# Eight PSUM banks handed out one or two at a time, and mask set-up moved to the front, in a planned attention + MLP kernel

## The chip, the cores and the metric

The kernel runs on one core of a Trainium2 chip. A time is the device time of one execution in microseconds. A "span" is the time from the first to the last instruction in a profile; it is about 1.8 us shorter than the time of the same execution.

## The reference

The reference is attention over 4 batches, 8 heads, 768 rows and 64 columns per head, with a local window of 96 keys and 8 global keys, followed by an MLP whose activation is h - tanh(h).

```
scores = q @ k^T / sqrt(64) - slope[head] * distance        # distance is |row - key|, 96 for far global keys
keep   = key < 8  or  0 <= row - key < 96
a      = softmax(where(keep, scores, -1e9))
x      = (a @ v) laid out as [4*768 rows, 8*64 columns]     # 3072 x 512
h      = x @ w_in                                           # 512 x 2048
out    = (h - tanh(h)) @ w_out                              # 2048 x 512, float32
```

## The kernel before

The work is cut into 24 units u, each one batch and 128 rows. A unit goes through these steps:

- T: k and q are transposed, on TensorE (PE) for the first 8 units and by a DMA transpose for the rest.
- B, S: the bias and the scores, one matmul group each. E: exp. From unit 3 on there is no B, and M multiplies by a mask that was made once (mk, mke).
- AV: probabilities times v. R: division by the sum.
- X: x is transposed, on PE for the first 9 units; from unit 9 on a DMA transpose on the SP queue does it (`a_DX`).
- m1, th, g, m2: the MLP.

A function `plan()` holds assumed durations of every operation and lists them in order of a simulated time. Each engine then executes its operations strictly in that order. So a change of buffers or of priorities moves instructions all over the kernel.

```
    ps_big = ctx.enter_context(tc.tile_pool(name="ps_big", bufs=2, space=bass.MemoryType.PSUM))   # 2 x two banks
    ps_one = ctx.enter_context(tc.tile_pool(name="ps_one", bufs=4, space=bass.MemoryType.PSUM))   # 4 x one bank
    ...
    def a_mk(m, a):
        mkp[m, a] = ps_one.tile([P, 512], FP32, name="one")
        bias(mkp[m, a], m, a, True)
    ...
    def a_DX(u):
        nc.sync.dma_start_transpose(out=x_dst(u), in_=xs[u].rearrange("q h d -> q (h d)"))
    ...
    SLACK_DT, SLACK_DX = 5.0, 2.0          # what the plan adds to a DMA transpose of k,q and of x
    LOADS = "tttiiiitiitoooiotoiooot"      # t: k, q, v of one unit; i: a piece of w_in; o: of w_out
    ...
        if u == 0:
            op(("ident",), POOL, 0.3, unit, after=[("issue", prev)])
            op(("nums",), POOL, 0.7, numbers, after=[("issue", ("ident",))])
    ...
    for h in range(H):
        eng = DVE if h < 2 else ACT
        op(("sl", h), eng, 0.14 if h < 2 else 0.22, lambda h=h, eng=eng: slope(h, eng), after=[("ident",)], pri=-3)
    ...
            op(("mk", m, a), PE, 0.22, lambda m=m, a=a: a_mk(m, a), after=biased_by + [("dT", 1), ("AV", 1)],
               take=["one"], pri=1)
    ...
        op(("R", u), DVE, 0.8, lambda u=u: a_R(u), after=[("AV", u)], take=["x"], give=["big"])
        b, at, n_b = block_of(u)
        xdep = ("Xe", u - 1) if at else None          # none for the first unit of a block
        ...
            op(("Xe", u), SP, 0.2, lambda u=u: a_DX(u), after=[("R", u), xdep],
               take=xtake, give=["x"], dma=T_DX, slack=SLACK_DX)
    ...
            op(("m1", g, f), PE, ..., after=[("Xe", us[-1]), ("in", (f + m - 1) // FJ)], take=["one"], pri=2, ...)
```

The softmax here doesn't subtract the row's maximum and nothing guards it: scores larger than these inputs give would overflow.

## Time and profile before

| | before |
|---|---|
| median of the runs, us | 217.36 (217.12 to 217.69) |
| span of the profiled run, us | 215.3 |
| PE busy | 208.8 us, 97% |
| VectorE, ScalarE busy | 61%, 59% |
| start of the first matmul, end of the last | 1.3 us, 212.0 us |

The first fence is from the page of the kernel before: the span, the busy times, the busy tenths of PE and of the DMA engines in 40 equal slices, and the share of each engine in the chain of work that ended last.

```profile
span 215.3 us, 5039 instructions
PE 208.8 (97%) x2031; PEld 127.3 (59%) x2031; DVE 132.3 (61%) x279; ACT 127.3 (59%) x214; POOL 72.0 (33%) x92
PE   6997999999999999999999999999999999999993
DMA  6999999999999999999999999226242011101112
PE 90%; DMA 4%; POOL 4%; issue 0%; DVE 0%; POOLq 0%
```

PE is full in nearly every slice after the fourth. What is lost is lost early, and the DMA engines are full until about 130 us. The next fence is the start of the chain of the kernel before. Its columns are the start in us, the length in us, and what it was.

```profile
9.38 8.14 DMA kq<-in_k_dram
17.52 0.04 issue
17.57 0.63 PE one L254 x8
```

The chain comes to the load of unit 3's k, which lands at 17.52 us, and after it there is almost only PE. The waits view of the kernel before gives PE's wait for this load. Its columns are the engine and line, what it waited for, us in all, times, and the longest. The second line, of POOL: the loads of k wait for a free buffer until a DMA transpose has read the old one.

```profile
PE one L254 <- DMA kq<-in_k_dram: 1.1, 1, 1.1
POOL kq L218 <- DMA qk<-kq: 36.8, 7, 7.9
```

**A measure used below: lost time.** For every matmul that computes something (warm-up matmuls left out) take its columns at 2.4 GHz, and at least 29.2 ns, close to the 29 to 30 ns at which the 65-column matmuls follow one another in this trace (median and mean within a group). The sum is 202.5 us, the same in all kernels here. Lost time at t is t less the needed work done by then, counting every matmul whose weight load has started except the last one. I read it from the starts of the weight loads, one for each matmul, because no record of these is missing (2031 here). It is good to about 0.2 us, the length of one 512-column matmul. A PE wait shows as a jump in lost time. A difference of lost time between two kernels is a lead of one over the other. In the kernel before it is 9.34 us at 24 us and 9.13 us at 208 us: from 24 us on PE loses nothing.

### The profile page before, as it was taken

The page shows a single profiled execution, that of the slowest core. Times are in us where ns is not written, and L with a number is a line of the kernel's source. Part 1 is how long each engine was busy: PE and PEld are TensorE (multiplying, and loading weights), DVE is VectorE, ACT ScalarE, POOL GpSimd, SP SyncE. Part 2 cuts the span into 40 slices and gives each one's busy share as a digit, 9 for nine tenths or more (in the row PEclk, how much of TensorE's full clock was granted, in tenths as well). Part 3 has the DMA queues.
Part 4 walks back from the last instruction along what each step waited for, and adds up shares of the span by engine and source line. Part 5 has one row for each costly group of instructions (what it writes and reads, how often), then busy time and mean ns, then how long its engine had stood idle before and what let it go on. Part 6 is the DMA issues. An engine that isn't in the chain of part 4 may idle for free.

```text
span 215.3 us, 5039 instructions
## 1 busy us (share of the span) xinstructions
PE 208.8 (97%) x2031; PEld 127.3 (59%) x2031; DVE 132.3 (61%) x279; ACT 127.3 (59%) x214; POOL 72.0 (33%) x92
## 2 busy tenths in 40 slices
PE   6997999999999999999999999999999999999993
PEld 1755996877745655455655655555555555555453
DVE  5555986759544889448878755766756644444311
ACT  5677998556543786536775655777477454434310
POOL 8976768698445354041354130000000000000000
PEclk9999999999999999999999999999999999999999
DMA  6999999999999999999999999226242011101112
GB/s 161 197 197 176 196 183 201 159 187 140 161 163 190 160 156 183 149 206 156 127 100 129 140 116 195 59 73 51 85 110 74 16 61 49 44 8 49 49 53 99
DMA packets 103960, 26.95 MB, mean 125 GB/s; under 512 B 92416, under 2 KB 100992, under 8 KB 103936
## 3 DMA queue, kind: packets, MB, share of 16 engines
q0 software_dynamic: 74048, 13.11, 80.0%
q1 hardware_dynamic: 26032, 6.95, 22.1%
q10 hardware_dynamic: 3856, 6.56, 9.3%
q8 instruction: 16, 0.26, 0.5%
q14 instruction: 8, 0.07, 0.1%
HBM read 27.26 MB, written 6.29 MB: 156 GB/s over the span
## 4 chain that ended last, share of the span: by engine, by line
PE 90%; DMA 4%; POOL 4%; issue 0%; DVE 0%; POOLq 0%
PE one L372 39%; PE one L404 39%; PE big L287 5%; DMA kq<-in_k_dram 4%; PE big L311 3%; PE big L315 2%; POOL w_in_bf L225 1%; POOL vb L212 1%; PE one L250 1%; PE one L338 1%; POOL kq L216 1%; PE one L254 1%; PE one L141 0%; POOL over L106 0%; POOL dist L106 0%
## 5 line engine op out<-in xcount | busy, mean ns | idle before, releaser
L372 PE MATMUL one<-xT,w_in_bf 128*128 128x128 bf16 (+1 forms) x768 | 96.7, 273 | 0.0
L404 PE MATMUL one<-w_out_bf,g 128*128 128x512 bf16 (+2 forms) x416 | 95.0, 363 | 0.0
L389 DVE TENSOR_TENSOR g<-one,th 128x384 bf16<-128x384 f32 (+1 forms) x120 | 67.7, 580 | 34.8 <-ACT th L383 32.6
L383 ACT ACTIVATE th<-one 128x384 f32<-128x384 f32 (+1 forms) x120 | 60.4, 516 | 43.3 <-PE one L372 39.5
L372 PEld LDWEIGHTS <-w_in_bf 128*128 128x128 bf16 x768 | 58.4, 98 | 29.3
L404 PEld LDWEIGHTS <-g 128*128 128x128 bf16 x416 | 37.9, 98 | 33.9
L218 POOL DMA_DIRECT2D kq<-in_k_dram x20 | 17.8, 891 | 40.7 <-DMA qk<-kq 36.8
L295 ACT ACTIVATE pd<-big 128x1024 bf16<-128x1024 f32 x24 | 24.6, 1024 | 7.9 <-PE big L287 7.9
L212 POOL DMA_DIRECT2D vb<-in_v_dram x24 | 21.6, 899 | 4.0 <-DMA qk<-kq 1.4
L298 DVE TENSOR_TENSOR pd<-pd,mk 128x1024 bf16<-128x1024 bf16 x21 | 14.5, 690 | 12.8 <-ACT pd L295 12.8
L295 ACT ACTIVATE po<-big 128x1024 bf16<-128x1024 f32 x20 | 20.5, 1027 | 0.5 <-PE big L287 0.5
L414 ACT COPY ot<-one 128x512 f32<-128x512 f32 x18 | 10.5, 585 | 15.7 <-PE one L404 15.7
L218 POOL DMA_DIRECT2D kq<-in_q_dram x20 | 17.7, 887 | 4.6 <-DMA vb<-in_v_dram 3.8
L324 DVE TENSOR_TENSOR x<-big,rden 128x512 bf16<-128x512 f32 x24 | 16.6, 691 | 0.8
L287 PEld LDWEIGHTS <-qk 64*128 64x128 bf16 x352 | 10.0, 94 | 8.6 <-issue 7.4
L287 PE MATMUL big<-qk 64*128 64x128 bf16 x352 | 14.4, 218 | 0.0
L311 PE MATMUL big<-vb,pd 128*128 128x65 bf16 x192 | 14.0, 193 | 0.2 <-ACT po L295 0.2
L298 DVE TENSOR_TENSOR po<-po,mk 128x1024 bf16<-128x1024 bf16 x18 | 12.4, 689 | 2.9 <-ACT po L295 2.9
L311 PEld LDWEIGHTS <-pd 128*128 128x128 bf16 x192 | 12.6, 97 | 2.0
L315 PE MATMUL big<-vb,po 128*128 128x65 bf16 x160 | 12.4, 193 | 0.0
L315 PEld LDWEIGHTS <-po 128*128 128x128 bf16 x160 | 10.4, 97 | 1.7 <-issue 0.2
L414 DVE COPY ot<-one 128x512 f32<-128x512 f32 (+2 forms) x8 | 4.5, 558 | 8.5 <-PE one L404 8.5
(45 smaller groups left out, 86.2 us busy)
## 6 DMA issues: line engine op xcount, KB each, us to landing
out_dram<-ot ACTq DMA_DIRECT2D x23, 256.0 KB, 2.9
vb<-in_v_dram POOLq DMA_DIRECT2D x24, 128.0 KB, 7.9
kq<-in_k_dram POOLq DMA_DIRECT2D x22, 128.0 KB, 8.1
kq<-in_q_dram POOLq DMA_DIRECT2D x22, 128.0 KB, 7.9
w_in_bf<-in_moe_w_in_dram POOLq DMA_DIRECT2D x8, 256.0 KB, 7.7
w_out_bf<-in_moe_w_out_dram POOLq DMA_DIRECT2D x8, 256.0 KB, 8.6
kf<-in_k_dram SPq DMA_DIRECT2D x2, 256.0 KB, 4.9
qf<-in_q_dram ACTq DMA_DIRECT2D x2, 256.0 KB, 3.8
```

Source lines behind the costliest of these rows:

```text
L212: i = nc.gpsimd.dma_start(out=vb[u % NV][:, :, 0:Dh], in_=by_head)
L218: i = nc.gpsimd.dma_start(out=dst.rearrange("p (h d) -> p h d", d=Dh), in_=by_head)
L287: nc.tensor.matmul(s[:, slot(2 * p + hh), :], qk[u - o][r, 1, p, :], qk[u][r, 0, p, :], start=u >= BIASED, stop=True, skip_group_check=u < ...
L295: nc.scalar.activation(pr[u, o], s, AF.Exp, bias=0.0, scale=scale)
L298: nc.vector.tensor_tensor(out=pr[u, o], in0=pr[u, o], in1=mk[:, :, mask_of(u, o), :], op=ALU.mult)
L311: nc.tensor.matmul(dst, pr[u, 0][:, slot(h), :], vb[u % NV][:, h, :], start=True, stop=last,)
L315: nc.tensor.matmul(dst, pr[u, 1][:, slot(h), :], vb[(u - 1) % NV][:, h, :], start=False, stop=True,)
L324: nc.vector.tensor_tensor(out=xs[u].rearrange("q (a h) d -> q a h d", a=2), in0=t[:, :, :, 0:Dh], in1=rden.to_broadcast([P, 2, H // 2, Dh] ...
L372: nc.tensor.matmul(t[:, (f - f0) * n : (f - f0 + 1) * n], w_in_bf[j][:, c, fo : fo + P], xT[b][:, c, o : o + n], start=(c == 0), stop=(c = ...
L383: nc.scalar.activation(h_view(ths[g, f0], g), h_view(hs[g, f0], g), AF.Tanh, bias=0.0, scale=1.0)
L389: nc.vector.tensor_tensor(out=gs[b][:, f0 : f0 + m, o : o + n], in0=h_view(hs.pop((g, f0)), g), in1=h_view(ths.pop((g, f0)), g), op=ALU.su ...
L404: nc.tensor.matmul(os_[u, part][:, 0 : hi - lo], gs[b][:, f, t * P : (t + 1) * P], w_out_bf[f // FJ][:, f % FJ, lo:hi], start=(f == 0), st ...
```

## The change

The intent: let any free bank, or any two adjacent ones, serve any use, so that the order of work is not held by the split into 2 two-bank and 4 one-bank buffers; make the positions and the identity before the first load of v, the slopes all on VectorE, and two of the three masks at once; and so start the dense stretch of PE earlier. A few assumed durations in `plan()` change too. The diff, cut to its core:

```diff
-    ps_big = ctx.enter_context(tc.tile_pool(name="ps_big", bufs=2, space=bass.MemoryType.PSUM))
-    ps_one = ctx.enter_context(tc.tile_pool(name="ps_one", bufs=4, space=bass.MemoryType.PSUM))
+    ps_pool = ctx.enter_context(tc.tile_pool(name="ps_pool", bufs=1, space=bass.MemoryType.PSUM))
+    NB = 8
+    ps = ps_pool.tile([P, NB, 512], FP32, name="ps")
+    banks = {}
+    def one(key):
+        return ps[:, banks[key], :]
+    def two(key):
+        return ps[:, banks[key] : banks[key] + 2, :]
 ... every user takes one(key) or two(key); take/give of "one" and "big" become hold/free of a key
-    LOADS = "tttiiiitiitoooiotoiooot"
+    LOADS = "tttiiiitiitoooiootiooot"
+    op(("ident",), POOL, 0.3, unit)
+    op(("nums",), POOL, 0.7, numbers, after=[("issue", ("ident",))])
+    prev = ("nums",)
-        if u == 0:
-            op(("ident",), POOL, 0.3, unit, after=[("issue", prev)])
-            op(("nums",), POOL, 0.7, numbers, after=[("issue", ("ident",))])
-            prev = ("nums",)
-        eng = DVE if h < 2 else ACT
-        op(("sl", h), eng, 0.14 if h < 2 else 0.22, lambda h=h, eng=eng: slope(h, eng), after=[("ident",)], pri=-3)
+        op(("sl", h), DVE, 0.12, lambda h=h: slope(h), after=[("ident",)], pri=-3)
-            op(("mk", m, a), PE, 0.22, ..., after=biased_by + [("dT", 1), ("AV", 1)], take=["one"], pri=1)
+            op(("mk", m, a), PE, 0.22, ..., after=biased_by + [("dT", 1), None if m else ("AV", 4)],
+               hold=[(("mk", m, a), 1)], pri=1)
 ... in plan(): the two pools are replaced by the times at which each bank is free
+        def find(hold):
+            got, at, b = {}, 0.0, list(bank)
+            for label, n in hold:
+                if n == 1:
+                    w, i = min((max(b[i], at), -i) for i in range(NB))
+                    i = -i
+                else:
+                    w, i = min((max(b[i], b[i + 1], at), i) for i in range(NB - 1))
+                ...
```

Not in the diff, because it follows from the plan: PE's order, and the times at which everything is issued, differ in the whole kernel.

More of the change, by code (lines that the diff above doesn't have):

```diff
@@ L88, with one_bf @@
     zero = cpool.tile([P, 512], BF16, name="zero")
+    NB = 8
[3 more added lines that the diff above has]
+        return ps[:, banks[key], :]
+    def one_bf(key):
+        return one(key).bitcast(BF16)
+    def two(key):
+        return ps[:, banks[key] : banks[key] + 2, :]
     w_in_bf = [cpool.tile([P, CD, FJ * P], BF16, name=f"w_in_bf{j}") for j in range(WJ)]
@@ L129, in distance_1, with slope @@
         nc.vector.memset(dT[:, 2, 0:G], float(L))
-    def slope(h, eng):
-        f = -(2.0 ** (-8.0 * (h + 1) / H)) / scale
-        if eng is ACT:
-            nc.scalar.activation(slopes[:, slot(h), :], ident, AF.Copy, bias=0.0, scale=f)
-        else:
-            nc.vector.tensor_scalar(
-                out=slopes[:, slot(h), :], in0=ident, scalar1=f, scalar2=None, op0=ALU.mult
-            )
+    def slope(h):
+        nc.vector.tensor_scalar(
+            out=slopes[:, slot(h), :], in0=ident, scalar1=-(2.0 ** (-8.0 * (h + 1) / H)) / scale,
+            scalar2=None, op0=ALU.mult,
+        )
     def bias(dst, m, a, stop):
@@ L148, in a_mk @@
     def a_mk(m, a):
-        mkp[m, a] = ps_one.tile([P, 512], FP32, name="one")
+        mkp[m, a] = one(("mk", m, a))
         bias(mkp[m, a], m, a, True)
@@ L166, in copy_on, with op @@
         return {ACT: nc.scalar.copy, DVE: nc.vector.tensor_copy, POOL: nc.gpsimd.tensor_copy}[eng]
-    def op(key, eng, us, fn, after=(), take=(), give=(), pri=0, dma=0.0, alt=None, at=None, slack=0.0):
+    def op(key, eng, us, fn, after=(), take=(), give=(), hold=(), free=(), pri=0, dma=0.0, alt=None, at=None, slack=0.0):
         ops[key] = dict(
             key=key, at=at, slack=slack, eng=eng, us=us, fn=fn, alt=alt, after=[a for a in after if a is not None],
-            take=list(take), give=list(give), pri=pri, dma=dma,
+            take=list(take), give=list(give), hold=list(hold), free=list(free), pri=pri, dma=dma,
         )
@@ L240, in a_T @@
         if u < APART or j == 1:
-            tr[u, j] = ps_one.tile([P, 2, NP, P], BF16, name="one")
+            tr[u, j] = one_bf(("T1" if j else "T", u)).rearrange("p (j n f) -> p j n f", j=2, f=P)
         else:
@@ L274, in a_B @@
     def a_B(u, o):
-        sc[u, o] = ps_big.tile([P, 2, 512], FP32, name="big")
+        sc[u, o] = two(("S", u, o))
         for a in range(2):
@@ L281, in a_S @@
             if u >= BIASED:
-                sc[u, o] = ps_big.tile([P, 2, 512], FP32, name="big")
+                sc[u, o] = two(("S", u, o))
             s = sc[u, o].rearrange("q a (h f) -> q (a h) f", f=P)
@@ L305, in a_AV @@
     def a_AV(u):
-        av[u] = ps_big.tile([P, 2, 512], FP32, name="big")
+        av[u] = two(("AV", u))
         t = av[u][:, :, 0 : (H // 2) * (Dh + 1)].rearrange("q a (h d) -> q a h d", d=Dh + 1)
@@ L335, in a_X @@
         x = xs[u].rearrange("q h d -> q (h d)")
-        tr[u, "x"] = ps_one.tile([P, CD, P], BF16, name="one")
+        tr[u, "x"] = one_bf(("X", u))[:, 0 : CD * P].rearrange("p (c f) -> p c f", f=P)
         for c in range(CD):
@@ L353 @@
     gs, hs, ths, os_, ots = {}, {}, {}, {}, {}
-    warm_bank = []
     def shape1(g):
@@ L361, in warm @@
     def warm():
-        if not warm_bank:
-            warm_bank.append(ps_one.tile([P, 512], FP32, name="one"))
-        nc.tensor.matmul(warm_bank[0], zero[:, 0:P], zero, start=True, stop=True)
+        nc.tensor.matmul(ps[:, NB - 1, :], zero[:, 0:P], zero, start=True, stop=True)
     def m1(g, f0):
         b, o, n, m = shape1(g)
-        t = hs[g, f0] = ps_one.tile([P, 512], FP32, name="one")
+        t = hs[g, f0] = one(("m1", g, f0))
         for f in range(f0, f0 + m):
@@ L400, in m2 @@
         if qq == 0:
-            os_[u, part] = ps_one.tile([P, DM], FP32, name="one")
+            os_[u, part] = one(("m2", u, part))
         b, t, _ = block_of(u)
@@ L422 @@
     AHEAD = 5.5
+    INF = 1.0e9
+    NUDGE = {}
     SLACK_DT, SLACK_DX = 5.0, 2.0
@@ L431, with load @@
             n_of[c] += 1
-    prev = None
-    def load(key, us, fn, dma, after=(), take=()):
+    op(("ident",), POOL, 0.3, unit)
+    op(("nums",), POOL, 0.7, numbers, after=[("issue", ("ident",))])
+    prev = ("nums",)
+    def load(key, us, fn, dma, after=(), take=(), slack=0.1):
         nonlocal prev
-        op(key, POOL, us, fn, after=[prev and ("issue", prev)] + list(after), take=take, dma=dma)
+        op(key, POOL, us, fn, after=[prev and ("issue", prev)] + list(after), take=take, dma=dma, slack=slack)
         prev = key
@@ L455 @@
             load(key, 0.7 if rows else 0.88, lambda u=u, nm=nm: load_bf(u, nm), T_ROWS if rows else T_LD,
-                 after=after, take=["kq"] if nm == "kf" else [])
-        if u == 0:
-            op(("ident",), POOL, 0.3, unit, after=[("issue", prev)])
-            op(("nums",), POOL, 0.7, numbers, after=[("issue", ("ident",))])
-            prev = ("nums",)
-    op(("dT", 0), DVE, 1.0, distance_0, after=[("nums",)], pri=-2)
+                 after=after, take=["kq"] if nm == "kf" else [], slack=1.0 if u == PLAIN + 1 else 0.15)
+    op(("dT", 0), DVE, 1.2, distance_0, after=[("nums",)], pri=-2)
     op(("dT", 1), DVE, 0.6, distance_1, after=[("nums",), ("issue", ("dT", 0))], pri=-1)
     for h in range(H):
-        eng = DVE if h < 2 else ACT
-        op(("sl", h), eng, 0.14 if h < 2 else 0.22, lambda h=h, eng=eng: slope(h, eng), after=[("ident",)], pri=-3)
+        op(("sl", h), DVE, 0.12, lambda h=h: slope(h), after=[("ident",)], pri=-3)
     biased_by = [("dT", 0)] + [("sl", h) for h in range(H)]
@@ L482 @@
         for a in range(2):
-            op(("mk", m, a), PE, 0.22, lambda m=m, a=a: a_mk(m, a), after=biased_by + [("dT", 1), ("AV", 1)],
-               take=["one"], pri=1)
+            op(("mk", m, a), PE, 0.22, lambda m=m, a=a: a_mk(m, a), after=biased_by + [("dT", 1), None if m else ("AV", 4)],
+               hold=[(("mk", m, a), 1)], pri=1)
             op(("mke", m, a), ACT, 0.52, lambda m=m, a=a: a_mke(m, a), after=[("mk", m, a)],
-               give=["one"], pri=1)
+               free=[("mk", m, a)], pri=1)
     for u in range(NU):
@@ L498 @@
             t_us = 0.47 if PLAIN <= u < ROWS else 0.24
-            two = u < APART
+            apart = u < APART
             for j, r in ((1, rk), (0, rq)):
                 prior = [("issue", ("T1", u))] if j == 0 else []
-                op(("T1" if j else "T", u), PE, t_us, lambda u=u, j=j: a_T(u, j), after=[r] + late + prior,
-                   take=["one"] if two or j else [], give=[] if j else ["kq"])
+                name = ("T1" if j else "T", u)
+                op(name, PE, t_us, lambda u=u, j=j: a_T(u, j), after=[r] + late + prior,
+                   hold=[(name, 1)] if apart or j else [], give=[] if j else ["kq"])
                 flex(("Te", u, j), [(ACT, 0.5), (DVE, 0.6 if u < ROWS else 0.34)],
                      lambda eng, u=u, j=j: a_Te(u, j, eng),
-                     after=[("T1" if j and two else "T", u)] + ([] if two or j else [("Te", u, 1)]),
-                     give=["one"] if two or not j else [])
+                     after=[("T1" if j and apart else "T", u)] + ([] if apart or j else [("Te", u, 1)]),
+                     free=[name] if apart else [] if j else [("T1", u)])
         else:
@@ L517 @@
                                     ("issue", ("B", u, 0) if o else ("S", u - 1, 0)) if u or o else None],
-                   take=["big"])
+                   hold=[(("S", u, o), 2)])
                 op(("S", u, o), PE, 0.43, lambda u=u, o=o: a_S(u, (o,)),
@@ L522 @@
             op(("S", u, 0), PE, 0.65 if i else 0.43, lambda u=u, os=os: a_S(u, os),
-               after=te + [kdep], take=["big"] * len(os))
+               after=te + [kdep], hold=[(("S", u, o), 2) for o in os])
         for o in os:
             op(("E", u, o), ACT, 0.93, lambda u=u, o=o: a_E(u, o), after=[("S", u, o if u < BIASED else 0)],
-               take=["p%d" % o], give=["big"])
+               take=["p%d" % o], free=[("S", u, o)])
             if u >= BIASED:
@@ L535 @@
            after=[(pm, u, 0), (pm, u, 1) if i else None, rv, ("V", u - 1) if i >= 2 else None],
-           take=["big"], give=["p0", "p1"] if i else ["p0"])
-        op(("R", u), DVE, 0.8, lambda u=u: a_R(u), after=[("AV", u)], take=["x"], give=["big"])
+           hold=[(("AV", u), 2)], give=["p0", "p1"] if i else ["p0"])
+        op(("R", u), DVE, 0.8, lambda u=u: a_R(u), after=[("AV", u)], take=["x"], free=[("AV", u)])
         b, at, n_b = block_of(u)
@@ L541 @@
         if u < PE_X:
-            op(("X", u), PE, 0.23, lambda u=u: a_X(u), after=[("R", u)], take=["one"], give=["x"])
+            op(("X", u), PE, 0.23, lambda u=u: a_X(u), after=[("R", u)], hold=[(("X", u), 1)], give=["x"])
             flex(("Xe", u), [(DVE, 0.34), (ACT, 0.5)], lambda eng, u=u: a_Xe(u, eng),
-                 after=[("X", u), xdep], take=xtake, give=["one"])
+                 after=[("X", u), xdep], take=xtake, free=[("X", u)])
         else:
@@ L553 @@
             op(("m1", g, f), PE, CD * m * (n / 2400.0 + 0.0025), lambda g=g, f=f: m1(g, f),
-               after=[("Xe", us[-1]), ("in", (f + m - 1) // FJ)], take=["one"], pri=2,
+               after=[("Xe", us[-1]), ("in", (f + m - 1) // FJ)], hold=[(("m1", g, f), 1)], pri=2,
                give=["xT"] if f + m == CF and end_b else [])
@@ L558 @@
             op(("g", g, f), DVE, 0.06 + 1.05 * w, lambda g=g, f=f: m1_g(g, f), after=[("th", g, f)],
-               take=["g"] if f == 0 and b else [], give=["one", "th"], pri=2)
+               take=["g"] if f == 0 and b else [], give=["th"], free=[("m1", g, f)], pri=2)
     for u in range(NU):
@@ L568 @@
                after=[("out", (4 * qq + 3) // FJ), ("g", g, (4 * qq + 3) // m * m)],
-               take=(["one", "mo"] if u < EARLY2 else ["one"]) if qq == 0 else [],
+               take=["mo"] if u < EARLY2 and qq == 0 else [], hold=[(("m2", u, part), 1)] if qq == 0 else [],
                give=["g"] if n == n_u - 1 and u >= N0 and u % HT == (N0 + HT - 1) % HT else [], pri=2)
@@ L574 @@
                  after=[("m2", u, 4 * part + 3)], take=["ot"] if part == 0 else [],
-                 give=["one", "mo"] if u < EARLY2 else ["one"], pri=1)
+                 give=["mo"] if u < EARLY2 else [], free=[("m2", u, part)], pri=1)
             op(("st", u, part), SP if u == NU - 1 else ACT, 0.1 if u == NU - 1 else 0.4, lambda u=u, part=part: store(u, part), after=[("ev", u, part)],
@@ L580, in plan @@
     def plan():
-        bufs = {"big": 2, "one": 4, "mo": 3, "kq": KQ, "p0": 3, "p1": 3,
+        bufs = {"mo": 3, "kq": KQ, "p0": 3, "p1": 3,
                 "x": 3, "xT": 3, "g": 3, "th": 3, "ot": 4}
         avail = {n: [0.0] * c for n, c in bufs.items()}
-        free = {PE: WARM[0], ACT: 2.8, DVE: 1.5, POOL: 0.85, SP: 0.7}
-        avail["one"][0] = WARM[1]
+        free = {PE: WARM[0], ACT: 3.4, DVE: 1.5, POOL: 1.2, SP: 0.7}
+        bank = [0.0] * NB
+        bank[NB - 1] = WARM[1]
+        def find(hold):
[6 more added lines that the diff above has]
+                    w, i = min((max(b[i], b[i + 1], at), i) for i in range(NB - 1))
+                if w == INF:
+                    return None, None
+                at, got[label] = w, i
+                b[i : i + n] = [INF] * n
+            return at, got
         ring = {SP: [0.0, []], POOL: [5.7, []]}
         share = {SP: 0.35, POOL: 0.65}
-        done, start = {}, {}
+        done, start, width = {}, {}, {}
         f1 = f2 = 0.0
@@ L627, in plan @@
                     continue
+                if o["hold"]:
+                    w = find(o["hold"])[0]
+                    if w is None:
+                        continue
+                    t = max(t, w)
                 for p in set(o["take"]):
@@ L635, in plan @@
                     continue
-                c = (round(t, 3), o["pri"], n)
+                c = (round(t + NUDGE.get(key, 0.0), 3), o["pri"], n)
                 if best is None or c < best[0]:
@@ L661, in plan @@
                 done[key] = end + LAT[o["eng"]]
+            if o["hold"]:
+                for b in range(NB):
+                    if bank[b] < t:
+                        bank[b] = t
+                got = find(o["hold"])[1]
+                banks.update(got)
+                for label, n in o["hold"]:
+                    bank[got[label] : got[label] + n] = [INF] * n
+                    width[label] = n
+            for label in o["free"]:
+                bank[banks[label] : banks[label] + width[label]] = [done[key]] * width[label]
             for p in o["take"]:
```

## The prediction

> **What bounds the kernel now.** TensorE: the page gives PE 208.8 of 215.3 us (97%) at full granted clock, VectorE 61%, ScalarE 59%. I summed every matmul's streamed columns at 2.4 GHz, warm-up matmuls left out: 201.7 us of needed work. The Trainium skill ("TensorE: Matmul & The Clock Gate", Back-to-back issue gap) gives N/2.4 + 2.5 ns per matmul; the trace agrees (four 512-column matmuls start every 0.86 us). From 20 us to the end the start-to-start gaps sum to about nothing: PE is dense. All that is lost is lost before: PE starts at 1.3 us, and up to 20 us only 10.7 us of needed work runs; the rest is 11 warm-up matmuls and waits.
>
> The waits view names the largest: 1.1 us of PE for the kq load of unit 3. In the chain of waits this load is the long piece, 9.38 to 17.52 us, and PE alone follows it. The POOL queue's loads land one after another, 0.9 to 1.3 us apart, from 7.3 to 40 us, with DMA at 9 tenths in the slices. So the end is "landing of a load + all PE work that stands behind it". For unit 3's k: 17.52 + (201.75 - 8.54) = 210.7 us, the highest of all loads; the last matmul ended at 212.0 (1.3 us[...] on top), the span at 215.3.
>
> **What the change does.** No work is added or removed: same 2031 matmuls, loads, evictions (six slopes move from ScalarE, where they took 1.3 us, to VectorE, about 0.15 us each). It moves work:
> - Positions and identity come before the first v load: bias ready at most 0.2 us earlier (4.6 to 4.4), since all slopes now precede the distances on VectorE.
> - Four mask matmuls and their exps come at 5 us instead of 14 to 20. ScalarE keeps 13 to 17 us for the exps of unit 2, so its second exp (16.7 us) comes about 1.6 us earlier, and AV of unit 2 with it. The first exp is delayed about 0.3 us (7.6 to 8.0).
> - With eight banks on demand three score tiles and an AV tile can stand at once.
> - PE's order as built: before unit 3's k transpose 11.1 us of needed work instead of 8.5 (masks, AV 2, X 2, two more MLP chunks). Its bound falls to 208.2.
>
> The same sum for every load, new order, old landings: the second w_out load (26.75 us, with 19.2 us of work before it, formerly 24.1) gives 209.3, the highest; the k loads of units 3 and 4, w_in 7 and later kq loads crowd at 208.2 to 208.9. So 210.7 falls to 209.3: 1.4 us. The loads cap it: a larger gain up front only waits for them. The tail (3.3 us from last matmul to end) is unchanged.
>
> **Prediction.** 216.0 us, range 214.9 to 217.2. Faster by over 2%: 0.02; within 2%: 0.96; slower by over 2%: 0.02.
>
> **What would show it.** Needed PE work before 20 us up from 10.7 to 12 us or more; no 1.1 us wait for kq of unit 3, but 0.5 to 1 us for w_out at 25 to 27 us; landings within 0.5 us of before; last matmul at about 210.5; same busy times.
>
> **What would make it wrong.** One PSUM tile making waits between unrelated banks (I saw none in the built order); early masks on ScalarE delaying the first scores more; a new hole after 30 us where PE, now ahead, waits for exps or loads; that w_out load landing later.

## More of the kernel before

From unit 6 on, three units form one block, and the first matmul of the block's m1 needs all three transposes of x.

`xdep` makes the plan put the transpose of x of a unit behind the planned landing of the one before it in the same block. The first unit of a block has no such condition. Units 9 to 11 are one block, and unit 12 begins the next. In the order that comes out, the transpose of unit 12 stands before that of unit 11 on the SP queue.

## The result, and the profile after

| | before | after |
|---|---|---|
| median, us | 217.36 | 217.22 (216.87 to 217.53) |
| ratio, 95% interval | | 0.9992 (0.9972 to 1.0012) |
| needed work done by 20 us, us | 10.66 | 11.89 |
| lost time at 24 us | 9.34 | 8.27 |
| lost time at 88 us | 9.45 | 8.17 |
| lost time at 104 us | 9.21 | 9.75 |
| end of the last matmul, us | 212.02 | 212.41 |

A ratio is the mean time of one kernel's fast runs over the mean of the other's in the same rounds, so it isn't quite the ratio of the medians quoted beside it. All outputs are right.

The time is the same. The table tells where it went: the kernel after leads by 1.1 us at 24 us and 1.3 us at 88 us, and has lost all of it, and 0.5 us more, by 104 us. The same lines of the page of the kernel after:

```profile
span 215.7 us, 5020 instructions
PE 208.0 (96%) x2005; PEld 127.5 (59%) x2031; DVE 132.3 (61%) x286; ACT 126.0 (58%) x207; POOL 71.9 (33%) x92
PE   7999999999999999988999999999999999999993
DMA  5999999999999999999999624323042021101112
PE 96%; issue 2%; DVE 1%; DVEq 0%
```

PE's fourth slice is now full. But there are two 8s, slices 18 and 19, about 92 to 102 us. A caution: this profile lacks 26 of PE's 2031 matmul records, and each missing one looks like a gap of about 0.2 us, so small gaps and the busy sum are not to be trusted here; the weight loads are all there. The chain of the kernel after, near those slices (start, length, what):

```profile
95.48 0.86 PE ps L409 x4
96.34 1.32 issue
97.67 3.41 PE ps L377 x20
```

And the first line of PE's waits in the kernel after:

```profile
PE ps L377 <- issue: 1.3, 1, 1.3
```

There is one wait of 1.3 us, before the first m1 matmul (L377) of the block of units 9 to 11, and the wait of 1.1 us for unit 3's k is gone. The profile calls the new wait "issue": it names no releaser. What the matmul waits for in the program are the three transposes of x of its block. So look at the last of them to be issued, unit 11's, on the SP queue. The view is of the tile xT on SP; the first line gives the time of the issue (ns, then start in us), the second the time from issue to landing. In the kernel before:

```profile
L350 SPq DMA_TRANSPOSE xT<-x x1: 1257/1257/1257, 88.8 to 88.8; - x1
DMA to landing us min/median/max: 5.3/5.3/5.3
```

And in the kernel after:

```profile
L358 SPq DMA_TRANSPOSE xT<-x x1: 1257/1257/1257, 88.7 to 88.7; - x1
DMA to landing us min/median/max: 8.9/8.9/8.9
```

In both kernels it is issued at 88.7 to 88.8 us. Before, it landed at 94.02 us, and PE came to it only at 95.92 us, as its timeline shows:

```profile
95.92 2.12 PE L372 MATMUL one<-xT,w_in_bf 128*128 128x384 bf16 x12
```

After, it landed at 97.58 us, and PE had come at 96.34 us and started at 97.67 us. So PE did not reach this matmul earlier than before: in the new order 1.3 us more needed work stands ahead of it. What makes the wait is that the landing moved by 3.6 us, more than the 1.9 us that it had to spare. So two things are to be explained: why a transpose whose data were ready at 86.14 us (the end of R of unit 11) was issued at 88.7, and why it then took 8.9 us.

For the first, the SP queue has unit 12's transpose ahead of it. VectorE's timeline in the kernel after has the ends of R of units 11 and 12 (start plus length):

```profile
85.45 0.69 DVE L332 TENSOR_TENSOR x<-ps,rden 128x512 bf16<-128x512 f32 x1
86.75 0.69 DVE L332 TENSOR_TENSOR x<-ps,rden 128x512 bf16<-128x512 f32 x1
```

So unit 12's transpose was issued at 87.47 us, and one transpose holds the queue for 1.2 us, as the first line of the view of xT shows. For the second, POOL issues the loads of unit 19 at about that time in the kernel after, and much later in the kernel before. The timeline of POOL, with start, length, line, and the idle time before it and its releaser, in the kernel before:

```profile
85.14 0.89 POOL L212 DMA_DIRECT2D vb<-in_v_dram  x1
92.56 0.88 POOL L218 DMA_DIRECT2D kq<-in_k_dram  x1 [6.53 <-DMA qk<-kq]
```

And in the kernel after, where the last three are the loads of unit 19 (the first line of each fence is unit 18's v):

```profile
84.69 0.90 POOL L220 DMA_DIRECT2D vb<-in_v_dram  x1
87.33 0.88 POOL L226 DMA_DIRECT2D kq<-in_k_dram  x1 [1.74 <-DMA qk<-kq]
88.19 0.89 POOL L226 DMA_DIRECT2D kq<-in_q_dram  x1
89.68 0.88 POOL L220 DMA_DIRECT2D vb<-in_v_dram  x1 [0.60 <-issue]
```

The loads come 5.2 us earlier, because unit 14's DMA transpose of k and q, which frees their buffer, was issued at 76.6 us instead of 83.1. The Trainium skill ("DMA: Bandwidth & Descriptors", Issuing engines are not separate DMA queues) says that transfers started from different engines run on the same 16 DMA engines and interleave; if so, these loads would slow the transpose. That has to be tested. The windows view of 88 to 98 us shows the cost in PE's busy time (columns: window, us, then busy time and count of PE, PEld, DVE, ACT, POOL, then granted clock, DMA share, GB/s), first in the kernel before:

```profile
88.00:98.00 10.00, 10.00 (x91) 5.23 (x89) 4.16 (x9) 5.21 (x8) 2.63 (x3) 1.00 1.77 176
```

And in the kernel after, where PE is busy 1.4 us less:

```profile
88.00:98.00 10.00, 8.63 (x81) 4.41 (x81) 5.45 (x12) 3.99 (x5) 1.96 (x3) 1.00 2.11 174
```

### The profile page after: what moved, and what is told of

Its sections match the earlier page's. It is cut to its first block, busy times and chain, and to the rows that moved or that the text cites. A ratio compares the mean times of both kernels' runs of the same rounds, so it can differ in the third digit from the quotient of the medians.

```text
span 215.7 us, 5020 instructions
## 1 busy us (share of the span) xinstructions
PE 208.0 (96%) x2005; PEld 127.5 (59%) x2031; DVE 132.3 (61%) x286; ACT 126.0 (58%) x207; POOL 71.9 (33%) x92
## 4 chain that ended last, share of the span: by engine, by line
PE 96%; issue 2%; DVE 1%; DVEq 0%
PE ps L377 39%; PE ps L409 38%; PE ps L295 6%; PE ps L319 3%; PE ps L323 2%; PE ps L149 2%; PE ps L369 2%; PE ps L258 2%; PE ps L346 1%; PE ps L262 1%; DVE x L332 0%; DVE ot L419 0%; DVE zero L736 0%; DVE rden L331 0%; DVE ident L735 0%
## 5 line engine op out<-in xcount | busy, mean ns | idle before, releaser
L377 PE MATMUL ps<-xT,w_in_bf 128*128 128x128 bf16 (+1 forms) x768 | 96.4, 273 | 1.4 <-issue 1.3
L409 PE MATMUL ps<-w_out_bf,g 128*128 128x512 bf16 (+2 forms) x391 | 92.0, 362 | 1.6 <-issue 0.5
L394 DVE TENSOR_TENSOR g<-ps,th 128x384 bf16<-128x384 f32 (+1 forms) x120 | 67.9, 581 | 38.0 <-ACT th L388 35.4
L388 ACT ACTIVATE th<-ps 128x384 f32<-128x384 f32 (+1 forms) x120 | 60.7, 515 | 51.0 <-PE ps L377 49.2
L377 PEld LDWEIGHTS <-w_in_bf 128*128 128x128 bf16 x768 | 58.2, 98 | 31.4 <-issue 2.0
L303 ACT ACTIVATE pd<-ps 128x1024 bf16<-128x1024 f32 x24 | 24.6, 1024 | 10.3 <-PE ps L295 10.3
L303 ACT ACTIVATE po<-ps 128x1024 bf16<-128x1024 f32 x20 | 20.5, 1023 | 0.0
L332 DVE TENSOR_TENSOR x<-ps,rden 128x512 bf16<-128x512 f32 x24 | 16.6, 691 | 0.8
L295 PE MATMUL ps<-qk 64*128 64x128 bf16 x352 | 14.4, 218 | 0.1
L319 PE MATMUL ps<-vb,pd 128*128 128x65 bf16 x192 | 14.1, 194 | 0.0
L323 PE MATMUL ps<-vb,po 128*128 128x65 bf16 x160 | 12.4, 194 | 0.0
```

What stands on the lines that cost most here:

```text
L295: nc.tensor.matmul(s[:, slot(2 * p + hh), :], qk[u - o][r, 1, p, :], qk[u][r, 0, p, :], start=u >= BIASED, stop=True, skip_group_check=u < ...
L303: nc.scalar.activation(pr[u, o], s, AF.Exp, bias=0.0, scale=scale)
L319: nc.tensor.matmul(dst, pr[u, 0][:, slot(h), :], vb[u % NV][:, h, :], start=True, stop=last,)
L323: nc.tensor.matmul(dst, pr[u, 1][:, slot(h), :], vb[(u - 1) % NV][:, h, :], start=False, stop=True,)
L332: nc.vector.tensor_tensor(out=xs[u].rearrange("q (a h) d -> q a h d", a=2), in0=t[:, :, :, 0:Dh], in1=rden.to_broadcast([P, 2, H // 2, Dh] ...
L377: nc.tensor.matmul(t[:, (f - f0) * n : (f - f0 + 1) * n], w_in_bf[j][:, c, fo : fo + P], xT[b][:, c, o : o + n], start=(c == 0), stop=(c = ...
```

## The experiments

The theory: the lead is real, and it is given back at one place, the transpose of unit 11, because of its place in the SP queue and of the loads beside it. The rivals: the change brings no lead that could reach the end (the eight banks alone, or the front alone, change nothing); or PE, being ahead, meets one late transfer after another, so that removing one wait only opens the next; or it is scatter. Eleven kernels were run in three jobs on three chips. Each was timed in five rounds beside the kernel before, whose medians were 217.18, 217.30 and 217.35 us.

### First job: the order on the SP queue, the loads, the banks alone

**after_swap.** The kernel after, with the transpose of unit 11 put just before that of unit 12. Nothing else moves.

```diff
     order, model_end = plan()
+    at = {key: t for t, key in order}
+    order = [(at["Xe", 12] - 0.0005 if key == ("Xe", 11) else t, key) for t, key in order]
```

> The changed kernel with one edit: on the SyncE queue the transpose of x of unit 11 goes before that of unit 12 (planner had it behind, though its input is ready 1.3 us earlier). Theory HOLE (the gain of 1.1 us at 20 us is kept to 96 us and lost in one PE wait for this transpose's landing at 97.6 us): issue falls from 88.7 to about 86.2 us, landing to before 96 us, the 1.3 us PE wait goes, 215.7 to 216.2 us. Rival SUPPLY (transfers as a whole cap PE until 130 us, so that a PE that is ahead meets another late transfer): wait moves to a later transfer, time stays at 216.9 or more.

Measured: 215.55 us (215.06 to 216.36), ratio 0.9929 (0.991 to 0.9948). The last matmul ended at 210.82 us. The transpose of unit 11 in the kernel with the swap:

```profile
L358 SPq DMA_TRANSPOSE xT<-x x1: 1190/1190/1190, 86.1 to 86.1; - x1
DMA to landing us min/median/max: 7.2/7.2/7.2
```

And its window of 88 to 98 us:

```profile
88.00:98.00 10.00, 10.00 (x91) 5.42 (x90) 6.00 (x13) 4.79 (x7) 2.08 (x3) 1.00 1.92 184
```

It is issued 2.6 us earlier and lands at 93.30 us, before PE comes; PE is full in the window. Lost time is 7.96 us at 88 us, 8.15 us at 104 us and 7.96 us at 208 us, so nothing is lost there and no new wait takes its place. The last matmul ends 1.6 us earlier than in the profile of the kernel after, and the lead reaches the end. In time, the swap is worth 0.6% by the ratios 0.9929 and 0.9992 (0.5% against the later second measurement of the kernel after, 0.9975, whose wider interval, 0.9941 to 1.0009, still touches that of the swap). The rival "one late transfer after another" falls for this kernel.

**after_gate.** The kernel after, with unit 12 still ahead of unit 11 on SP, but the three loads of unit 18 held until the transpose of unit 11 has landed. The aim was to hold the loads that start at 87.3 us. The edit does more: counted in the traces these loads are unit 19's, and the expectation below calls them unit 18's by mistake. The edit names unit 18, whose loads start at 83.0 us in the kernel after (83.4 us in the kernel before), and since POOL works in order, those of unit 19 wait behind them. So six loads are held.

```diff
-    gate_of = {}
+    gate_of = {("ld", "kf", 18): ("Xe", 11)}
-        nc.sync.dma_start_transpose(out=x_dst(u), in_=xs[u].rearrange("q h d -> q (h d)"))
+        i = nc.sync.dma_start_transpose(out=x_dst(u), in_=xs[u].rearrange("q h d -> q (h d)"))
+        dmas["Xe", u] = i
 ... after plan():
+    held = {("ld", nm, 18): at["Xe", 11] + 0.0001 * (n + 1) for n, nm in enumerate(("kf", "qf", "vf"))}
+    order = [(held.get(key, t), key) for t, key in order]
```

> The changed kernel with the order kept, but the three loads of unit 18 (k, q, v, issued at 87.3, 88.2, 89.7 us) wait until the transpose of x of unit 11 has landed. If those loads, which run earlier than before the change, are what stretched this transpose from 5.3 us to 8.9 us, it lands by about 94.0 to 94.8 us as before the change, the PE wait goes, and the time is 215.7 to 216.3 us. If they are not, the landing stays near 97.5 and the time near 217.2. Under SUPPLY the wait moves on and the time stays at 216.9 or more.

Measured: 215.99 us (215.12 to 216.98), ratio 0.9953 (0.9926 to 0.998). The gate held unit 18's loads to 95.69 us, as POOL's timeline shows, and unit 19's to 98.29 us. The view of xT on SP has the transpose of unit 11:

```profile
95.69 0.88 POOL L226 DMA_DIRECT2D kq<-in_k_dram  x1 [14.84 <-DMA xT<-x]
L358 SPq DMA_TRANSPOSE xT<-x x1: 1257/1257/1257, 88.5 to 88.5; - x1
DMA to landing us min/median/max: 6.7/6.7/6.7
```

The transpose was issued at 88.50 and landed at 95.17 us, 6.7 us later, not 94.0 to 94.8 as expected. PE's wait is gone (lost time 7.96 us at 88 us, 7.99 at 104). So in this profile, with both units' loads held, the wait is gone; one profile cannot tell this from the scatter of the landing that before_again shows below. In time it is less clear than the swap: this interval overlaps a little with that of the kernel after (0.9972 to 1.0012). It doesn't bring back the 5.3 us of the kernel before, which is a first sign that the loads are not the whole reason for the 8.9 us.

**before_swap.** The same swap in the kernel before, as a control: there the transpose had 1.9 us to spare.

> Control: the same swap of two transposes in the kernel before the change. There PE reached the first MLP matmul of units 9 to 11 1.9 us after the landing, so under HOLE nothing is won: 217.1 to 217.6 us, landing of unit 11 some 2 to 4 us earlier. If the swap itself helps whatever PE's lead is, it would be under 216.8.

Measured: 216.43 us (216.22 to 216.97), ratio 0.9971 (0.9954 to 0.9988). The transpose of unit 11 was issued at 84.64 instead of 88.76 us:

```profile
L350 SPq DMA_TRANSPOSE xT<-x x1: 2177/2177/2177, 84.6 to 84.6; - x1
DMA to landing us min/median/max: 8.9/8.9/8.9
```

It landed at 93.53 us, only 0.5 us earlier than before, not 2 to 4. And it took 8.9 us although here the loads of unit 19 were issued only from 91.77 us on. So these loads are not needed to make it slow. The control did not come out as "no effect": 0.3% was won. before_again, below, suggests why.

**psum_only.** The kernel after with its front undone: loads order, place of positions and identity, slopes on two engines, masks after AV of unit 1, and the plan's constants as before. Only the eight banks remain.

```diff
-    LOADS = "tttiiiitiitoooiootiooot"
+    LOADS = "tttiiiitiitoooiotoiooot"
-        op(("sl", h), DVE, 0.12, lambda h=h: slope(h), after=[("ident",)], pri=-3)
+        eng = DVE if h < 2 else ACT
+        op(("sl", h), eng, 0.14 if h < 2 else 0.22, lambda h=h, eng=eng: slope(h, eng), after=[("ident",)], pri=-3)
-               after=biased_by + [("dT", 1), None if m else ("AV", 4)],
+               after=biased_by + [("dT", 1), ("AV", 1)],
 ... ident and nums back behind the first load of v
```

> One part alone: one PSUM tile of eight banks on demand, with the kernel before's order of first loads, slopes, distances and masks (after the AV of unit 1). Its plan happens to put unit 11's transpose before unit 12's. If the eight banks give the early lead, PE has about 11.5 to 12 us of needed work done by 20 us (10.7 before, 11.9 with the whole change) and, with no wait near 97 us, the time is 216.0 to 216.6. If the lead comes from the masks and distances made first, work at 20 us stays near 10.7 and the time at 217.0 to 217.6.

Measured: 217.23 us (216.57 to 217.38), ratio 0.9998 (0.9981 to 1.0015). Needed work by 20 us is 11.03 us and lost time at 24 us 8.97, a lead of 0.37 us over the kernel before. Unit 3's k landed at 17.83 us, and PE still waited 0.7 us for it. By the times, eight banks alone win nothing. The profile is a poor measure of their lead: full clock came only at 7.11 us, against 4.14 us in the kernel before, and PE ended 0.4 us earlier (211.62 us), but the rest of the span took 3.9 us instead of 3.3.

### Second job: what is scatter, what the parts are worth

**before_again.** The kernel before with a comment added, so that the comparison measures itself.

> The kernel before the change against itself (a comment added): what one program loaded twice differs by. The control swap in the kernel before came out at a ratio of 0.9971, though PE's lead at 20 us, which the swap cannot touch, had already moved by 0.5 us with the landing of unit 3's k (16.96 us in place of 17.52). If that was the scatter of this landing, the ratio here is 1 within 0.003 and the landing of unit 3's k lies between 16.9 and 17.9 us. If the swap really won 0.3%, this ratio is within 0.001 of 1 and the landing at 17.5.

Measured: 217.24 us (217.11 to 217.98), ratio 1.0004 (0.9984 to 1.0023). The time is the same, but its profile isn't. Unit 3's k landed at 16.33 us, not at 17.52 and outside both expectations, so PE was ahead (lost time 8.97 us at 24 us against 9.34). Then the transpose of unit 11, issued at 88.4, took 7.5 us, landed at 95.89, and PE waited for it. PE's timeline in this kernel names the releaser:

```profile
95.94 1.31 PE L372 MATMUL one<-xT,w_in_bf 128*128 128x384 bf16 x7 [0.31 <-DMA xT<-x]
```

The last matmul ended at 212.04 us, as in the first profile of the same kernel (212.02). Two things follow. First, the floor at the transpose was in the kernel before as well, just hidden: in this run, what PE won early it lost there. That can explain why before_swap won 0.3%: its PE led by 0.5 us at 24 us and kept the lead. It is argued from one profile of each, not shown. Second, the same transpose of the same kernel took 5.3 us in one run and 7.5 us in another, with the loads of unit 19 starting at 92.3 to 92.6 us in both. So 2.2 us of the difference between 5.3 and 8.9 can be scatter.

**front_swap.** The kernel before, with its own PSUM pools, but with the whole front of the change and with the swap.

```diff
     ps_big = ...        # kept: 2 x two banks
     ps_one = ...        # kept: 4 x one bank
-    LOADS = "tttiiiitiitoooiotoiooot"
+    LOADS = "tttiiiitiitoooiootiooot"
 ... ident and nums first, all slopes on DVE, masks 1 and 2 without ("AV", 1), mask 0 after ("AV", 4)
+    order = [(at["Xe", 12] - 0.0005 if key == ("Xe", 11) else t, key) for t, key in order]
```

> The other part alone: distances, slopes and two masks first, with the old two PSUM pools (two of two banks, four of one), and unit 11's transpose ahead of unit 12's so that the late hole is not in play. If masks and positions first give the lead, PE has 11.7 us or more done by 20 us and the ratio is 0.993 to 0.995. If both parts are needed, about 11.0 to 11.4 us and 0.996 to 0.999.

Measured: 216.43 us (216.31 to 216.66), ratio 0.9962 (0.9944 to 0.998). The lead is there at first: 12.10 us of needed work by 20 us, lost time 7.90 us at 24 us. By 36 us lost time is 8.99 us. It goes in two places, half a microsecond in each: after 33 us, where PE's view shows a wait of 0.18 us for q of unit 5 (landed 33.45), and after 34 us, where it waits 0.46 us for a one-bank buffer to be emptied:

```profile
34.84 0.55 PE L369 MATMUL one<-xT,w_in_bf 128*128 128x128 bf16 x7 [0.46 <-ACT xT L344]
```

The kernels with eight banks have no such losses: after_swap's lost time is 8.17 us at 24 us and 8.28 at 32, and 8.51 at 40. So in these profiles the front makes the lead and the eight banks keep it. The work by 20 us is what was expected if the front alone were enough, the ratio what was expected if both parts are needed. The two kernels come from different jobs, and their intervals just touch (0.9944 to 0.998 against 0.991 to 0.9948).

**masks_late.** The kernel after, with the masks as before (after AV of unit 1), and the order on SP mended in the plan instead of after it: a transpose of x follows the issue, not the landing, of the one before it.

```diff
-            op(("Xe", u), SP, 0.2, lambda u=u: a_DX(u), after=[("R", u), xdep],
+            op(("Xe", u), SP, 0.2, lambda u=u: a_DX(u), after=[("R", u), xdep and ("issue", xdep)],
-               after=biased_by + [("dT", 1), None if m else ("AV", 4)],
+               after=biased_by + [("dT", 1), ("AV", 1)],
```

> Eight banks and positions first, but the masks after the AV of unit 1 again (and each transpose of x need not be planned behind the landing of the one before, which keeps unit 11 ahead of unit 12). In the three profiles with masks first the full clock came at 6.5 us, so the four masks at 4 us took 427 ns each and the first scores started at 8.5 us in place of 7.2. If the masks first are what gives the lead, work at 20 us falls to 11 us and the ratio rises to 0.996 to 1.0. If they only fill time that warm-up matmuls had anyway, work at 20 us stays at 11.7 to 12.2 and the ratio at 0.991 to 0.994.

Measured: 217.11 us (216.96 to 217.48), ratio 0.9991 (0.9974 to 1.0008). A miss, but an instructive one. The lead is there (lost time 7.74 us at 24 us, 7.96 at 88), and the order on SP is right (unit 11 issued at 85.6 us). But the plan now thinks that the transpose lands early and puts m1 of the block early too. It landed at 92.67 us, 7.07 us after its issue, and PE, idle from 91.40, started on it at 92.72. Lost time is 9.48 us at 104 us. Here PE's waits view does name it:

```profile
PE ps L377 <- DMA xT<-x: 1.3, 1, 1.3
```

**masks_mid.** As masks_late, but two masks come right after the first scores.

```diff
-               after=biased_by + [("dT", 1), None if m else ("AV", 4)],
+               after=biased_by + [("dT", 1), ("S", 0, 0) if m else ("AV", 4)],
 ... and the edit of ("Xe", u) as in masks_late
```

> As masks_late, but the four early masks after the first scores (they then run at the full clock, between AV 0 and the scores of unit 1). First scores at about 7.3 us, work at 20 us 12.0 to 12.5 us if the 1.3 us of half clock had cost the lead, ratio 0.988 to 0.992. If the landings of unit 3's k and of the second w_out load hold PE (the sum that I predicted by), it stays at 11.9 to 12.1 us and 0.992 to 0.994.

Measured: 215.40 us (215.11 to 215.47, 5 runs), ratio 0.991 (0.9892 to 0.9928), the lowest median of all. The lead (lost time 7.63 us at 24 us) reaches the end (last matmul at 210.25). But masks_late and masks_mid differ also in what the plan made of block 9 to 11, so this pair says nothing of the masks yet.

### Third job: the plan's slack, and the kernel after once more

**after_again.** The kernel after with a comment added.

> The changed kernel once more, unedited but for a comment. So far its late wait stands on one profile. HOLE: again a PE wait of 1 us or more at 95 to 98 us for the transpose of x of unit 11, ratio 0.998 to 1.001. If the first profile was an outlier: no wait, and a ratio of 0.993 to 0.996.

Measured: 216.92 us (216.04 to 218.61), ratio 0.9975 (0.9941 to 1.0009). The profiled run, the fastest of the six, had PE at full clock early and a bigger lead (lost time 7.21 us at 24 us). And it lost 1.2 us at the same place (7.11 us at 88 us, 8.31 at 104): PE sat idle for 1.06 us and went on at 96.25 us; the transpose, issued at 87.56, landed at 96.16 us, 8.6 us later. So the wait is no accident of one profile. The rest of that bigger lead reached the end: its last matmul ended at 210.99 us. The ratio lies just outside the 0.998 to 1.001 expected. The six runs scatter more than those of most kernels here, and the interval includes 1, as in the first measurement.

**late_slack.** masks_late, with the plan's slack for the landing of a transpose of x raised.

```diff
-    SLACK_DT, SLACK_DX = 5.0, 2.0
+    SLACK_DT, SLACK_DX = 5.0, 6.0
```

> masks_late, which met a wait of 1.5 us at 91.2 us though unit 11's transpose came first, with one number of the planner changed: it reckons a transpose of x to land 4 us later than it did (slack 6 in place of 2; the trace shows 5 to 9 us from issue to landing at 80 to 100 us). If the cause is that the plan places the first MLP matmul of units 9 to 11 before the landing, the plan now places it later, the wait goes, and the ratio falls from 0.9991 to 0.991 to 0.994. If transfers as a whole cap PE there, it stays at 0.997 or more.

Measured: 215.67 us (215.58 to 215.97), ratio 0.9917 (0.9896 to 0.9939); last matmul at 210.65 us. The transpose of unit 11 was issued at 85.48 and landed at 92.56 us, much as in masks_late, but now PE had other work until 95.04 us (lost time 7.96 us at 88 us, 7.88 at 104):

```profile
L358 SPq DMA_TRANSPOSE xT<-x x1: 1194/1194/1194, 85.5 to 85.5; - x1
DMA to landing us min/median/max: 7.1/7.1/7.1
```

Telling the plan that a transpose is slow is as good as making it early.

**mid_slack.** masks_mid with the same slack.

> masks_mid, the fastest so far, with the same number of the planner changed. It had no wait of over 0.35 us after 20 us, so nothing is left to win: ratio 0.989 to 0.993, the same as masks_mid. If its margin was luck of one plan, some rounds of masks_mid would have been slower; here the spread should be no wider.

Measured: 215.81 us (215.14 to 216.45), ratio 0.9917 (0.9892 to 0.9942). Its profiled run was its slowest, with a lost time of 8.59 us already at 24 us. In it full clock came only at 7.23 us, and the load of k issued at 3.78 us landed at 10.17 us, against 8.81 in masks_mid. The ratio counts, not this profile. The spread, expected to be no wider than that of masks_mid, was wider (1.3 us against 0.4). The pair late_slack and mid_slack, equal but for the masks, has the same ratio: where the masks stand gives nothing that five rounds can show.

The versions masks_mid, late_slack, mid_slack and after_swap are 0.7 to 0.9% under the kernel before, and their intervals overlap; the kernel after, measured twice, is at 0.9992 and 0.9975. after_swap needs the least: one line.

## Why the prediction was right or wrong

The prediction was 216.0 us (214.9 to 217.2). Measured were 217.22 us, the same as before within the interval, so the promised 1.4 us did not come. The class, within 2%, was right.

**Right: the lead up front.** Needed work by 20 us was to rise from 10.7 to 12 us or more; it rose to 11.89, just short. The wait of 1.1 us for unit 3's k is gone: PE has other work and comes to that transpose only at 19.38 us, when k has long landed at 16.44. The lead of 1.1 us at 24 us is nearly the gain that was predicted, and after_swap shows that it reaches the end when nothing takes it back (215.55 us; its last matmul at 210.8 against the predicted 210.5). That its size came out near the prediction is in part luck: the kernel before was profiled with full clock from 4.14 us, the kernel after only from 6.47 us, and in after_again, at full clock from 4.37 us, the lead at 24 us was 2.1 us. The tail is as said: 3.27 us.

**Wrong: "The same sum for every load, new order, old landings".** This is the step that failed. It had two faults, and the second decided.

- It was a sum over loads. The transposes of x on SP are DMA transfers too, and each has PE work behind it, but they were left out. Worked out the same way with 202.5 us of needed work, the kernel before has 17.52 + (202.49 - 8.59) = 211.4 us for unit 3's k, and 94.02 + (202.49 - 86.69) = 209.8 us for unit 11's transpose. So the transpose wasn't the limit in the profile at hand, but it was near.
- It took old landings. With its old landing the transpose would have given 94.02 + (202.49 - 88.01) = 208.5 us in the new order, and no alarm. It landed at 97.58 us, which gives 212.06 us, above the old limit, and the last matmul ended at 212.41. The prediction claimed landings within 0.5 us of before. This one moved by 3.6 us; unit 3's k moved by 1.1 us.

**Wrong: "From 20 us to the end PE is dense".** True of that one profile, but it was read as a property of the kernel. The second profile of the kernel before has a wait at 96 us. The prediction named "a new hole after 30 us where PE, now ahead, waits for exps or loads" as what would make it wrong. The hole came; it was neither an exp nor a load.

**Wrong in size or not seen.** The wait of 0.5 to 1 us for the second w_out load at 25 to 27 us isn't there, though the load landed at 26.83 us, where it was expected. The bias was ready earlier than predicted (first bias matmul at 3.85 us instead of 4.4). The first exp came at 8.95 us, not 8.0, and the second exp of unit 2 at 15.53 us, 1.2 us earlier than before instead of 1.6. The late first exp goes with the clock: in the profile of the kernel after, PE was at full clock only from 6.47 us, and the six early matmuls of bias and masks started 427 ns apart; in after_again it was at full clock from 4.37 us, and the first exp came at 7.99 us.

**What stays open.** Why unit 11's transpose took 8.9 and 8.6 us in the two profiles of the kernel after. The loads of unit 19, which come 5.2 us earlier, may have a part in it: with them and unit 18's held, it took 6.7 us and the wait was gone. But by the time alone that isn't clear (ratio 0.9953, against 0.9992 and 0.9975 for the kernel after, with overlapping intervals), after_gate held unit 18's loads too, and the kernel before has 5.3 and 7.5 us with the same loads at nearly the same times. Two more profiles speak against unit 19's loads as the main reason: with them issued only from 91.8 us (before_swap) and 91.4 us (front_swap) on, it took 8.9 and 9.5 us, and with them issued at 86 to 89 us in after_swap, masks_late and late_slack only 7.1 to 7.2. How much is other transfers and how much is scatter between executions is not settled. That PE's stop at this transpose takes the gain is settled: moving the transpose (after_swap) and telling the plan of its slowness (late_slack against masks_late, 0.9917 against 0.9991) both take the stop away and bring the gain.

## What to carry to other kernels

When a change brings the bottleneck engine forward, list every transfer that it will meet, DMA transposes between on-chip buffers too, and give each its margin: landing less the time at which the engine comes. A margin smaller than the gain, or than what the landing can move by (here 1.9 us against 3.6), can cap the gain. In a planned kernel, check the order on the slow queues by hand, and tell the plan the landing times that the trace shows at that place, here 7 us and more.

## What the Trainium skill lacked or had wrong

- "DMA: Bandwidth & Descriptors", Latency and other measured facts: the page gives an effective bandwidth of a DMA transpose, 261 to 400 GB/s. From that I would estimate 0.3 to 0.5 us for moving the data of a 128x512 bf16 tile (131 KB), without any fixed cost. From issue to landing such a tile took 2.3 to 8.9 us in the kernel after (median 3.6), and issuing one held the SP queue for 1.2 us (once 2.3). The time of such a transpose beside other transfers is not on the page.
- The same page, Issuing engines are not separate DMA queues: that transfers of different engines interleave fits after_gate (8.9 us in the kernel after, 6.7 us with six loads held, one profile each), but these runs do not show it by themselves: before_swap took 8.9 us with unit 19's loads issued only in its last 1.8 us. The page says nothing of how much the landing of one transpose varies. The same transpose of one unchanged kernel took 5.3 and 7.5 us in two runs.
- "TensorE: Matmul & The Clock Gate", Back-to-back issue gap: the formula N/2.4 + 2.5 ns agrees (216 ns for 512 columns: four in 0.86 us in the chain above). The section says that this formula over-counts at large N in real streams, 131 ns for 512 columns. These runs don't show that: in a stream with a weight load for each matmul the gap stays at 216 ns.
- The same page, What you observe: the section lets the clock's change vary by 500 ns to either side. That is too narrow for this kernel: here the same program reached full clock at 6.47 us in one profile and at 4.37 us in another, 2.1 us apart, and the lost time at 24 us differed by 1.06 us.
